# Routing 36 tiles in six groups of six instead of nine of four, over a two-group ring of rows, with GpSimd's early low halves issued in a row

## The chip, the cores and the metric

The kernel runs on one core of a Trainium2 chip. The metric is device microseconds of one execution: the median of three executions for the kernel as it is timed, and one more execution that the hardware profiler took, from which every row below comes.

## What is computed

Attention with keys and values pooled by eight feeds a mixture of eight experts with one expert per token. Cut to what matters:

```python
def reference(q, k, v, w_gate, w_output_gate, w1, w2):     # q, k, v: (8, 8, 576, 64)
    k_p = k.reshape(B, H, Sp, 8, D).mean(axis=3)           # 72 pooled keys
    v_p = v.reshape(B, H, Sp, 8, D).mean(axis=3)
    attn = softmax(q @ k_p^T / 8)
    x = (attn @ v_p).transpose(0, 2, 1, 3).reshape(4608, 512)
    logits = x @ w_gate                                    # (4608, 8)
    e_idx = argmax(logits);  gate_w = softmax(logits)[e_idx]
    eom = sigmoid(x @ w_output_gate)
    for e in range(8):                                     # w1: (8, 512, 1024), w2: (8, 1024, 512)
        mask = e_idx == e
        out[mask] = gate_w[mask] * eom[mask, e] * (relu(x[mask] @ w1[e]) @ w2[e])
```

## The kernel before

The 4608 tokens are 36 tiles of 128. The program has two parts, with a barrier of all engines between them.

**The first part** is one instruction stream that was recorded by a Python loop over `i` in 0 to 38, two halves (`a`) a step. There is no scheduler behind it: the instructions of each engine stand in the order in which the loop issued them, every engine takes its own in that order, and semaphores hold one back until what it reads is written. In half-step `a` of step `i` the loop issues the scores of tile `i` (TensorE, `scores`, L328), the transposes of the probabilities of tile `i-2` (`transpose_p`, L349, copied out by ScalarE, L350), the negated row maxima of tile `i` (VectorE, `peak`, L334, tiles `m`), the product with the values of tile `i-3` (`values`, L360), the four exponentials (ScalarE, `softmax`, L340) and the normalising of tile `i-3` into the row buffer `xg` (`normalise`, VectorE, L377 and L383). A dictionary `plan` holds other work by step: loading and pooling keys (GpSimd adds, L260, then ScalarE's `scale_k`, L265, into `kbd`), halving the values (GpSimd, L282), and so on. A row of `xg` holds a token's attention output, its id and its gate weight.

**Routing** works on a group of tiles. When the last tile of a group is normalised, `route(g)` is put into a queue two steps later; `work` then takes a few VectorE instructions from it in each half-step, among the others. The first reduces the gate columns of the group's rows (L398), some twelve small ones follow, TensorE counts ranks with 1 + n matmuls (L435, L437), and the last of them, a cast (L460), writes `where`: the place of each token in a buffer `xs` in HBM that is sorted by expert. From then on `place_ids` issues one indirect DMA (a scatter) for each tile from GpSimd's queue (L514), one a half-step; at the end of the loop whatever is left goes out at once. A group's rows in `xg` are free again when their scatters have landed. The scatters have their numbers by tile, 0 to 35.

**The first layer of expert 0** starts inside the first part. When 24 tiles are placed, `gather_early` (step 31) loads three tiles of `xs` (SyncE, L105). `turn_x` transposes each (VectorE, L110), `turn_hi` copies it to the high half of `xt` (ScalarE, L556), and `turn_lo` writes the low half (GpSimd, L560, three instructions). The early pieces of `w1` are split in the same way: `split_hi` (ScalarE, L539) and `split_lo` (GpSimd, L543, eight instructions of 128x512), at the steps in `HIGHS` and from 31.5 on every half-step. After the loop a list `TAIL` says the order by hand: `M` is a hidden chunk on TensorE (`hidden_chunk`, L732, twelve matmuls, which need the high and low halves of all three tiles), `W10` ten pieces of routing work, `Z` one more indirect DMA that puts blank rows behind the first expert's (`blank_tail`, L472), `Y` an output chunk (L738). The rank matmuls of the last group stand on TensorE behind two `M`.

**The second part** (`experts`) runs all experts by loops over jobs of two or three tiles. Before it SyncE waits until every scatter and the blank tail have landed, and all engines meet at a barrier (L1685 in the profile). Five of the eight output chunks `Y` stand before the barrier, the others behind it.

Of the kernel before, what the change touches and what calls it, by code (L numbers as in the profile page):

```python
# [10 lines left out]
F32 = mybir.dt.float32  # L11
# [11 lines left out]
P = 128  # L23
# [14 lines left out]
ROW = ID + 2  # L38
# [2 lines left out]
SENT_ID = SENT - 2  # L41
PAIRS = SENT // 2
LOADS = 4 * 16
GROUPS = (4,) * 9
TAKEN = 5
BEFORE = 31
TURNS = 33.5
SIDES = ((0, 5), (5, 3))
# [34 lines left out]
TURN = 5  # L83
FIRST = 2
HIGHS = (21, 25, 25.5, 26, 29.5, 30, 30.5, 33)
PLACED = (0, 1, 1, 2, 2, 3, 3)
SOONER = 192
CODE = 159
# [35 lines left out]
def attention_and_routing(ctx, tc, sh, qT, kT, v, wg, wst, xs):  # L124
    nc = tc.nc
    cp = ctx.enter_context(tc.tile_pool(name="cp", bufs=1))
    p2 = ctx.enter_context(tc.tile_pool(name="p2", bufs=2))
# [3 lines left out]
    def const(shape, dt, name):  # L131
        return cp.tile(shape, dt, tag=name, name=name)
# [186 lines left out]

    s_t, pT_t, xg, grec = {}, {}, {}, {}  # L320
    GMAX = max(GROUPS)
    place = [(g, j) for g, n in enumerate(GROUPS) for j in range(n)]

    def scores(i, a):
# [27 lines left out]
    def values(i, a):  # L352
        av = sh.p_y[a]
        pT = pT_t[i]
        for c, k_a, k0, k1 in side_slots():
            if k_a != a:
                continue
            o = COLS * (SLOTS[k0][2] - SIDES[a][0])
            for r0, n, b, s0 in segments(i):
                nc.tensor.matmul(av[r0:r0 + n, o:o + COLS * (k1 - k0)], pT[:, BLOCKS[0] * a + c, r0:r0 + n],  # L360
                                 vbd[b % 2][:, k0:k1].rearrange("p h f -> p (h f)"),
                                 start=(c == 0), stop=(c == BLOCKS[a] - 1), skip_group_check=True)
        g, j = place[i]
        if a == 0:
            if j == 0:
                while len(placed) < sum(GROUPS[:max(g - 2, 0)]):
                    work(1, True)
                    place_ids()
                xg[g] = p2.tile([P, GMAX, ROW], F32, tag="xg", name=f"xg{g}", bufs=3)
                n, t0 = group(g)  # L370
                nc.gpsimd.iota(xg[g][:, 0:n, ID], pattern=[[P, n]], base=t0 * P, channel_multiplier=1,
                               allow_small_or_imprecise_dtypes=True)
                grec[g] = p2.tile([P, GMAX, H], F32, tag="grec", name=f"grec{g}")
        h0, n = SIDES[a]
        hs = slice(h0, h0 + n)
        avv = av[:, 0:n * COLS].rearrange("p (h f) -> p h f", h=n)
        nc.vector.reciprocal(grec[g][:, j, hs], avv[:, :, COLS - 1])  # L377
        return avv
# [7 lines left out]
    def group(g):  # L386
        return GROUPS[g], sum(GROUPS[:g])

    def small(g, shape, dt, name):
        whole = [P, GMAX + shape[1] - GROUPS[g]] + shape[2:]  # L390
        return p2.tile(whole, dt, tag=name, name=f"{name}_{g}", bufs=1)[:, 0:shape[1]]
# [115 lines left out]
    todo, placed = [], []  # L507
# [91 lines left out]
    def at(step, f, *args):  # L599
        plan.setdefault(step, []).append((f, args))  # L600
# [8 lines left out]
    def work(n, force=False):  # L609
        while n > 0 and queue:  # L610
            for item in queue:
                if force or item[1] <= tick[0]:
                    hold = next(item[0], None)
                    if hold is None:
                        queue.remove(item)
                    else:
                        item[1] = tick[0] + hold
                        n -= 1
                    break
            else:  # L620
                return

    for b in range(1, B):
        f = S * b // P + 0.5 * (b % 2)
# [23 lines left out]
        at(18 + 3 * c, stage_in, c)  # L648
    for c in range(8):
        at(HIGHS[c], split_hi, c)  # L650
        at(31.5 + 0.5 * c, split_lo, c, 0, nc.gpsimd)
    for g in range(len(GROUPS)):
        at(sum(GROUPS[:g + 1]) + 2, lambda g: queue.append([route(g), 0, g]), g)

# [1060 lines left out]
```

## Time and profile before

| | |
|---|---|
| median of three executions | 582.61 us (580.53 to 583.93) |
| the profiled execution | 585.02 us |
| its span in the trace | 583.1 us |
| TensorE (PE) busy | 566.6 us, 97% of the span |
| VectorE (DVE), ScalarE (ACT), GpSimd (POOL) busy | 335.9, 252.9 and 238.1 us |
| granted TensorE clock, mean | 0.995 |

A busy share is a mean over both parts. The rows further down are therefore taken by stretch: from the start to about 136 us the attention loop runs in full, from there to 146 us it runs out, and the first part ends at the barrier at about 168 us. In a timeline row the columns are the start, the duration, the engine, the line, the operation with its tiles, the number of instructions merged, and in brackets how long the engine was idle before and who ended it. A q behind an engine's name is its sequencer.

### The profile page before, as it was taken

How to read it: one execution, taken by the hardware profiler on the slowest of the kernel's cores; microseconds unless marked ns; L12 is line 12 of the kernel's file. 1: busy time of each engine (PE TensorE's matmuls, PEld its weight loads, DVE VectorE, ACT ScalarE, POOL GpSimd, SP SyncE). 2: the span in 40 equal slices, each digit the busy share in tenths (PEclk: the TensorE clock that was granted, in tenths of full speed). 3: DMA queues.
4: the chain of work that ended last, by engine and by line, in shares of the span. 5: the costliest groups of instructions: out<-in, count | busy, mean ns of one | idle time of the engine just before them, and what ended most of it. 6: DMA issues, size and time to landing. Idle time of an engine off the chain costs nothing.

```text
span 583.1 us, 12099 instructions
## 1 busy us (share of the span) xinstructions
PE 566.6 (97%) x3381; PEld 513.8 (88%) x3382; DVE 335.9 (58%) x771; ACT 252.9 (43%) x686; POOL 238.1 (41%) x361
## 2 busy tenths in 40 slices
PE   6999999998989999999999999999999999999996
PEld 6899998987978989898989898898998998989895
DVE  4788898888868616688665342646263741413231
ACT  2898899996425204564444120424142420302120
POOL 6658999859625422155223131231212421212131
PEclk9899999999999999999999999999999999999999
DMA  8968899967866712589772413256132212020202
GB/s 333 331 244 299 295 373 369 337 192 207 252 179 219 242 63 59 189 265 301 261 240 95 149 28 82 46 188 183 47 87 95 60 38 69 0 72 18 63 27 73
DMA packets 50351, 97.22 MB, mean 167 GB/s; under 512 B 6686, under 2 KB 32414, under 8 KB 48608
## 3 DMA queue, kind: packets, MB, share of 16 engines
q1 hardware_dynamic: 42304, 77.18, 42.0%
q0 software_dynamic: 7968, 19.24, 9.4%
q14 instruction: 61, 0.50, 0.3%
q8 instruction: 18, 0.29, 0.2%
HBM read 75.12 MB, written 22.59 MB: 168 GB/s over the span
## 4 chain that ended last, share of the span: by engine, by line
PE 56%; issue 0%; DVE 0%; POOL 0%; DVEq 0%; POOLq 0%
PE p_y L1176 27%; PE p_h L1222 27%; PE p_h L1198 1%; PE p_y L1185 0%; PE p_h L1204 0%; PE p_y L1186 0%; POOL out L1629 0%; DVE rows L1420 0%; DVE ht L1428 0%; DVEq L911 0%; DVEq L901 0%; DVEq L1019 0%; DVEq L1008 0%; DVEq L1427 0%; DVEq L1488 0%
## 5 line engine op out<-in xcount | busy, mean ns | idle before, releaser
L1290 ACT ACTIVATE ht<-p_h 128x384 fp32r<-128x384 f32 (+1 forms) x104 | 46.7, 450 | 234.4 <-PE p_h L1222 217.5
L1629 POOL DMA_INDIRECT out<-rows,dst x41 | 43.2, 1054 | 194.1 <-DVE rows L1420 191.3
L1222 PE MATMUL p_h<-xt,w1b 128*128 128x384 f32 (+1 forms) x672 | 107.6, 320 | 0.5 <-issue 0.5
L1222 PEld LDWEIGHTS p_h<-xt,w1b 128*128 128x128 f32 x672 | 106.6, 189 | 1.5 <-issue 1.1
L1428 DVE SCALAR_TENSOR_TENSOR ht<-p_h,ht 128x384 fp32r<-128x384 f32 (+1 forms) x104 | 52.2, 503 | 92.3 <-ACT ht L1290 83.7
L1176 PE MATMUL p_y<-w2b,ht 128*128 128x512 f32 x456 | 104.8, 390 | 0.0
L1176 PEld LDWEIGHTS p_y<-w2b,ht 128*128 128x128 f32 x456 | 85.4, 188 | 17.5
L1176 PE MATMUL p_y<-w2a,ht 128*128 128x512 f32 x384 | 88.6, 390 | 0.0
L1222 PEld LDWEIGHTS p_h<-xt,w1a 128*128 128x128 f32 x576 | 84.8, 190 | 1.5 <-issue 0.7
L1222 PE MATMUL p_h<-xt,w1a 128*128 128x384 f32 (+1 forms) x576 | 85.9, 309 | 0.2
L1176 PEld LDWEIGHTS p_y<-w2a,ht 128*128 128x128 f32 x384 | 71.8, 188 | 15.0 <-issue 0.4
L1420 DVE TENSOR_SCALAR rows<-p_y,sc 128x512 f32<-128x512 f32 x37 | 27.7, 750 | 99.2 <-PE p_y L1176 91.1
L340 ACT ACTIVATE p<-p_h,m 128x72 f32<-128x72 f32 x288 | 73.0, 390 | 4.0 <-DVE m L334 3.0
L1606 POOL DMA_INDIRECT xm<-xs,src x54 | 58.0, 1073 | 26.4 <-POOL src L1602 13.5
L360 PE MATMUL p_y<-vbd,pT 128*128 128x162 f32 (+3 forms) x400 | 67.4, 319 | 0.3 <-DVE xg L383 0.2
L360 PEld LDWEIGHTS p_y<-vbd,pT 128*128 128x128 f32 (+1 forms) x400 | 54.0, 179 | 3.4 <-issue 0.7
L514 POOL DMA_INDIRECT xs<-xg,where x36 | 36.3, 1008 | 24.5 <-DVE grec L377 11.3
L260 POOL TENSOR_TENSOR kq<-kq 128x288 f32<-128x288 f32 (+1 forms) x59 | 37.4, 659 | 7.1 <-ACT p L340 3.9
L383 DVE TENSOR_TENSOR xg<-p_y,grec 128x400 f32<-128x400 f32 x72 | 36.2, 503 | 1.6
L350 ACT ACTIVATE pT<-ptr 128x384 f32<-128x384 f32 x72 | 35.7, 496 | 3.0 <-PE ptr L349 2.1
L334 DVE TENSOR_REDUCE m<-p_h 128x4 f32<-128x288 f32 x72 | 32.3, 449 | 4.4 <-PE p_h L328 1.9
L349 PE MATMUL ptr<-ident,p 128*128 128x128 f32 x180 | 32.6, 279 | 1.7 <-ACT pT L350 1.0
(191 smaller groups left out, 679.4 us busy)
## 6 DMA issues: line engine op xcount, KB each, us to landing
stage<-wst SPq DMA_DIRECT2D x64, 512.0 KB
kq<-kT SPq DMA_DIRECT2D x7, 1152.0 KB
rows<-xs SPq DMA_DIRECT2D x40, 192.0 KB
rows<-v SPq DMA_DIRECT2D x8, 768.0 KB
rows<-v SPq DMA_DIRECT2D x8, 512.0 KB
rows<-xs SPq DMA_DIRECT2D x64, 64.0 KB
q_even<-qT SPq DMA_DIRECT2D x3, 1152.0 KB
kq<-qT SPq DMA_DIRECT2D x3, 1152.0 KB
```

The lines of the kernel that those rows point to most:

```text
L260: nc.gpsimd.tensor_tensor(k[:, :, 0:w], k[:, :, 0:w], k[:, :, w:2 * w], op=ALU.add)
L340: nc.scalar.activation(pt[i % 3][:, o:o + KEYS], sv[:, h], AF.Exp, bias=m[:, h:h + 1])
L350: nc.scalar.activation(pT_t[i][:, BLOCKS[0] * a:BLOCKS[0] * a + n, :], tr[:, 0:P * n].rearrange("p (c n) -> p c n", c=n), AF.Copy)
L360: nc.tensor.matmul(av[r0:r0 + n, o:o + COLS * (k1 - k0)], pT[:, BLOCKS[0] * a + c, r0:r0 + n], vbd[b % 2][:, k0:k1].rearrange("p h f -> p ...
L383: nc.vector.tensor_tensor(view(xg[g][:, j], h0, [[H, D + 16], [1, n]]), avv[:, :, 0:D + 16].rearrange("p h f -> p f h"), grec[g][:, j, h0: ...
L514: ins = nc.gpsimd.indirect_dma_start(out=xs, out_offset=bass.IndirectOffsetOnAxis(ap=where, axis=0), in_=x.bitcast(I32), in_offset=None)
L1176: i = mm(to, ht[:, h, f, P * k:P * k + P], w[:, part, o:o + DM], start=(f == 0 and part == 0 and h == 0), stop=(f == 7 and h == 1))
L1222: i = mm(to, w[:, part, o:o + P], x, start=(d == 0 and k == 0), stop=(d == 3 and k == len(terms) - 1))
L1290: act(ht[:, 0, f, 0:n], p_h[f % 3][:, 0:n], AF.Relu).then_inc(q["hh"], 1)
L1428: nc.vector.scalar_tensor_tensor(ht[:, 1, f, 0:n], src, 0.0, ht[:, 0, f, 0:n].bitcast(F32), op0=ALU.max, op1=ALU.subtract).then_inc(q["hl" ...
L1606: nc.gpsimd.indirect_dma_start(out=xb[:, k].bitcast(I32), out_offset=None, in_=pairs_of, in_offset=bass.IndirectOffsetOnAxis(ap=src[:, k:k ...
L1629: nc.gpsimd.indirect_dma_start(out=out, out_offset=bass.IndirectOffsetOnAxis(ap=dst[:, k:k + 1], axis=0), in_=yb[2 if k == size - 1 else k ...
```

## The change

Routing takes six groups of six tiles in place of nine of four. The first 24 tiles are now groups 0 to 3, so `TAKEN` is 3 in place of 5. The rows lie in one buffer of two groups (12 tiles, as three groups of four were), and a row is written again as soon as the scatter of that one tile is through: `values` asks for the scatter of the tile twelve earlier, not for a whole group. The ids of a group (L371, an iota on GpSimd) are written with its last tile, not with its first. The table `LOWS` replaces 31.5, 32, 32.5 ... as the steps of GpSimd's eight low halves.

```diff
-GROUPS = (4,) * 9
-TAKEN = 5
+GROUPS = (6,) * 6
+TAKEN = 3
...
+LOWS = (31.5, 31.5, 32, 32, 32.5, 32.5, 33, 34)
...
     GMAX = max(GROUPS)
+    group_rows = const([P, 2, GMAX, ROW], F32, "xg")
...
         if a == 0:
-            if j == 0:
-                while len(placed) < sum(GROUPS[:max(g - 2, 0)]):
+            while g > 1 and len(placed) <= sum(GROUPS[:g - 2]) + j:
+                work(1, True)
+                place_ids()
+            n, t0 = group(g)
+            if j == n - 1:
+                while g > 1 and len(placed) < sum(GROUPS[:g - 1]):
                     work(1, True)
                     place_ids()
-                xg[g] = p2.tile([P, GMAX, ROW], F32, tag="xg", name=f"xg{g}", bufs=3)
-                n, t0 = group(g)
                 nc.gpsimd.iota(xg[g][:, 0:n, ID], pattern=[[P, n]], base=t0 * P, channel_multiplier=1,
                                allow_small_or_imprecise_dtypes=True)
+            if j == 0:
+                xg[g] = group_rows[:, g % 2]
                 grec[g] = p2.tile([P, GMAX, H], F32, tag="grec", name=f"grec{g}")
...
-        at(31.5 + 0.5 * c, split_lo, c, 0, nc.gpsimd)
+        at(LOWS[c], split_lo, c, 0, nc.gpsimd)
```

How the instructions stand on three places now. Lines from 83 on have higher numbers in the changed kernel: L514 is L520, L543 is L549, L560 is L566, L383 is L389, L460 is L466.

GpSimd at the end of the first part, before. The scatters (DMA) are tiles 25, 26 and 27 of group 6, then four of group 7 and four of group 8 (the first scatter of group 6 and four low halves stand ahead of these rows); `w1a` is a low half of a weight, `xt` the low half of a gathered tile.

```order
L514 DMA xs<-xg_1606,where_1949 38912x514
L543 TENSOR_TENSOR w1a<-stage,w1a 128x512
L514 DMA xs<-xg_1606,where_1949 38912x514
L543 TENSOR_TENSOR w1a<-stage,w1a 128x512
L371 IOTA xg_2064 128x4
L514 DMA xs<-xg_1606,where_1949 38912x514
L543 TENSOR_TENSOR w1a<-stage,w1a 128x512
L560 TENSOR_TENSOR xt<-rows,xt 128x4x128
L543 TENSOR_TENSOR w1a<-stage,w1a 128x512
L560 TENSOR_TENSOR xt<-rows,xt 128x4x128 x2
L514 DMA xs<-xg_1832,where_2160 38912x514 x4
L514 DMA xs<-xg_2064,where_2248 38912x514 x4
```

The same place now, from the first low half on; the scatters are tiles 24 to 29 of group 4 and 30 to 35 of group 5.

```order
L549 TENSOR_TENSOR w1a<-stage,w1a 128x512 x7
L220 MEMSET kbd_75 128x514
L221 MEMSET kbd_75 128x1
L549 TENSOR_TENSOR w1a<-stage,w1a 128x512
L520 DMA xs<-xg,where_1954 38912x514
L566 TENSOR_TENSOR xt<-rows,xt 128x4x128
L520 DMA xs<-xg,where_1954 38912x514
L566 TENSOR_TENSOR xt<-rows,xt 128x4x128
L520 DMA xs<-xg,where_1954 38912x514 x4
L566 TENSOR_TENSOR xt<-rows,xt 128x4x128
L375 IOTA xg 128x6
L520 DMA xs<-xg,where_2134 38912x514 x6
```

The low halves of the weights have moved ahead of the scatters, all six scatters of group 4 now stand ahead of the last `xt`, and the last group has six scatters in place of four.

VectorE near the end of the loop, before, from the second row maximum of tile 34 to the second of tile 35 (`m`); the routing rows (L398, L402, L404) begin group 7.

```order
L334 TENSOR_REDUCE m_1_2031<-p_h 128x4
L377 RECIPROCAL grec_1834<-p_y 128x3
L383 TENSOR_TENSOR xg_1832<-p_y,grec_1834 128x80x3
L110 STREAM_TRANSPOSE rows<-rows 128x4x4x32
L334 TENSOR_REDUCE m_0_2058<-p_h 128x4
L398 TENSOR_REDUCE routing<-xg_1832 128x64
L377 RECIPROCAL grec_2066<-p_y 128x5
L402 TENSOR_REDUCE mx_2068<-routing 128x4
L383 TENSOR_TENSOR xg_2064<-p_y,grec_2066 128x80x5
L404 TENSOR_TENSOR d_2069<-routing,mx_2068 128x32
L110 STREAM_TRANSPOSE rows<-rows 128x4x4x32
L334 TENSOR_REDUCE m_1_2091<-p_h 128x4
```

The same place now, from the same row maximum of tile 34 to the cast that ends the routing of group 4.

```order
L336 TENSOR_REDUCE m_1_1937<-p_h 128x4
L447 TENSOR_REDUCE routing<-ex_1851 128x6
L383 RECIPROCAL grec_1856<-p_y 128x3
L451 TENSOR_TENSOR routing<-routing,running 128x48
...
L111 STREAM_TRANSPOSE rows<-rows 128x4x4x32
L336 TENSOR_REDUCE m_0_1977<-p_h 128x4
L460 SCALAR_TENSOR_TENSOR grec__4_1946<-ez_1892,routing 128x6
L461 TENSOR_REDUCE at_1953<-routing 128x6
L383 RECIPROCAL grec_1856<-p_y 128x5
L465 RECIPROCAL xg<-grec__4_1946 128x6
L466 CAST where_1954<-at_1953 128x6
```

Where group 7 began, group 4 of the changed kernel now ends: five routing instructions (L447, L451, L452, L454, L455) stand between the two maxima, and the cast that the scatter of tile 24 waits for follows the first maximum of tile 35; before, that cast (of group 6) stood in front of the first maximum of tile 34.

GpSimd in the middle of the loop, before, around the adds (`kq`) that pool the keys of batch 3 and the values (`rows`).

```order
L260 TENSOR_TENSOR kq<-kq 128x288 x2
L514 DMA xs<-xg_290,where_565 38912x514
L260 TENSOR_TENSOR kq<-kq 128x288 x2
L514 DMA xs<-xg_290,where_565 38912x514
L260 TENSOR_TENSOR kq<-kq 128x144 x2
L514 DMA xs<-xg_290,where_565 38912x514
L260 TENSOR_TENSOR kq<-kq 128x144 x2
L514 DMA xs<-xg_290,where_565 38912x514
L260 TENSOR_TENSOR kq<-kq 128x4x72
```

The same adds now.

```order
L261 TENSOR_TENSOR kq<-kq 128x288 x4
L261 TENSOR_TENSOR kq<-kq 128x144 x4
L261 TENSOR_TENSOR kq<-kq 128x4x72
L283 TENSOR_TENSOR rows<-rows 128x64x4 x3
L520 DMA xs<-xg,where_655 38912x514
L283 TENSOR_TENSOR rows<-rows 128x64x4 x2
L520 DMA xs<-xg,where_655 38912x514 x4
```

The first group's scatters no longer stand among the adds of batch 3 but behind them.

## Rows read from the trace of the kernel before

**Rows 1.** Busy time by stretch: start:end, length, then PE, PEld, DVE, ACT, POOL.
```profile
20.00:136.00 116.00, 113.94 (x915) 104.47 (x914) 98.44 (x348) 107.08 (x420) 91.79 (x131) 1.00 0.83 295
136.00:146.00 10.00, 8.36 (x57) 7.20 (x56) 8.43 (x35) 4.59 (x16) 9.48 (x10) 1.00 0.82 236
```

**Rows 2.** Timeline of PE, from the end of attention to the second part.
```profile
143.86 0.44 PE L732 MATMUL p_h<-xt,w1a 128*128 128x384 f32 x1
145.26 4.26 PE L732 MATMUL p_h<-xt,w1a 128*128 128x384 f32 x23 [0.95 <-POOL xt L560]
...
167.94 7.79 PE L738 MATMUL p_y<-w2a,ht 128*128 128x512 f32 x33 [1.59 <-PEq L1685]
```

**Rows 3.** Timeline of POOL at the end of the first part.
```profile
130.43 0.99 POOL L514 DMA_INDIRECT xs<-xg,where  x1 [5.91 <-DVE grec L377]
...
133.51 1.00 POOL L514 DMA_INDIRECT xs<-xg,where  x1 [0.16 <-issue]
...
143.06 2.15 POOL L560 TENSOR_TENSOR xt<-rows,xt 128x512 fp32r<-128x512 f32 x2
145.52 0.99 POOL L514 DMA_INDIRECT xs<-xg,where  x1 [0.32 <-DVE where L460]
146.81 0.96 POOL L514 DMA_INDIRECT xs<-xg,where  x1 [0.30 <-issue]
...
153.14 0.96 POOL L514 DMA_INDIRECT xs<-xg,where  x1 [2.83 <-issue]
...
156.94 1.82 POOL L514 DMA_INDIRECT xs<-xg,where  x1 [0.30 <-DVE ht L594]
159.07 0.96 POOL L472 DMA_INDIRECT xs<-kbd,tail_at x1 [0.30 <-issue]
```

**Rows 4.** What SyncE's sequencer waited for: us in total, times, longest.
```profile
SPq L1685 <- DMA xs<-kbd,tail_at: 1.6, 1, 1.6
SPq L1685 <- DMA stage<-wst: 0.7, 1, 0.7
```

**Rows 5.** Groups by line: the reduction that opens a group's routing.
```profile
L398 DVE TENSOR_REDUCE routing<-xg 128x64 f32<-128x512 f32 x9 | 6.2, 684 | 0.0
```

**Rows 6.** Timeline of DVE in steps 33 to 36: routing, row maxima, turning, a late cast.
```profile
127.24 0.20 DVE L441 TENSOR_REDUCE routing<-ex 128x4 f32<-128x32 f32 x1
127.47 0.20 DVE L445 TENSOR_TENSOR routing<-routing,running 128x32 f32<-128x32 f32 x1
...
129.57 0.45 DVE L334 TENSOR_REDUCE m<-p_h 128x4 f32<-128x288 f32 x1
...
130.01 0.14 DVE L460 CAST where<-at 128x4 int32<-128x4 f32 x1
...
132.80 0.70 DVE L110 STREAM_TRANSPOSE rows<-rows 128x512 f32<-128x512 f32 x1
133.42 0.42 DVE L334 TENSOR_REDUCE m<-p_h 128x4 f32<-128x288 f32 x1
...
134.93 0.42 DVE L334 TENSOR_REDUCE m<-p_h 128x4 f32<-128x288 f32 x1
...
143.70 1.53 DVE L460 CAST where<-at 128x4 int32<-128x4 f32 x1
```

**Rows 7.** Who waited for whom: ACT's copies of pooled keys for GpSimd's adds.
```profile
ACT kbd L265 <- POOL kq L260: 3.7, 2, 1.8
```

**Rows 8.** Busy time in the two stretches around those waits, columns as in rows 1.
```profile
50.00:55.00 5.00, 4.95 (x43) 4.43 (x42) 4.07 (x18) 3.11 (x13) 4.81 (x9) 1.00 0.82 317
66.00:71.00 5.00, 5.00 (x48) 4.14 (x47) 3.98 (x19) 3.12 (x14) 4.97 (x9) 1.00 0.72 287
```

**Rows 9.** The scatters' line: time from issue to landing.
```profile
DMA to landing us min/median/max: 5.0/7.5/7.7
```

**Rows 10.** Timeline of SyncE: the early gather of three tiles.
```profile
123.08 1.87 SPq L105 DMA_DIRECT2D rows<-xs  x4
```

## The prediction

> **What bounds the kernel now.** I read the busy time by stretch first. In the attention loop, from 20 to 136 us, PE is busy for 113.94 of 116 us [rows 1]; ACT with 107.08 and DVE with 98.44 are near it but not it. All that PE lacks there is 2.06 us, so whatever the change saves on DVE, ACT or POOL in the loop cannot give back more than that. From 136 to 146 us, where the loop runs out, PE is idle for 1.64 of 10 us, and POOL, with 9.48 busy, is the fullest engine [rows 1].
>
> Then the timeline of PE at the two seams. At 143.86 it issues the first matmul of the first layer, and then stands for 0.95 us until GpSimd has written the last low half of `xt`; it goes on at 145.26 [rows 2], and POOL's row for the last two `xt` ends at 143.06 + 2.15 = 145.21 [rows 3]. So POOL's order of work at the end of the loop already sets the time there. From 145.26 on PE is never idle for long until the barrier: it is out of work at 167.94 - 1.59 = 166.35, and goes on at 167.94 [rows 2]. SyncE holds the barrier until the last indirect DMA (the blank tail, issued at 159.07 [rows 3]) and a weight load have landed: it waited 1.6 us for the one and a further 0.7 us for the other [rows 4]. Behind the barrier PE is the chain to the end, so a microsecond lost at either seam arrives at the end.
>
> **The change part by part.**
>
> *Fewer, larger groups.* The routing's small instructions on DVE, ACT and PE come six times in place of nine; the opening reduction grows from 512 to 768 elements, by its mean of 684 ns [rows 5] to about 1.0 us (an estimate, by size). On DVE this frees several us, but DVE is not what PE waits for. The bounds are a gain of 2.06 us, if all of PE's idle time in the loop were due to it, and a loss of 0.5 us, if the longer reduction or a later add holds up a row maximum. PE does not show a wait at each of the nine groups, so I take a quarter of the upper bound: **-0.5 us**.
>
> *POOL in the middle of the loop.* The first group's scatters no longer stand among the adds of batch 3. ACT waited for those adds twice, 1.84 us each time, 3.7 in total [rows 7]; these waits should go. But in the two stretches that hold them PE was busy for 4.95 and 5.00 of 5 us [rows 8]: the tiles ahead of ACT covered the wait. I cost it at nothing beyond the -0.5. With that cover gone it would be worth 3.7 us (a rival, below).
>
> *The ring.* A row is written again twelve tiles later, as before. By the order, each row's scatter is issued at least three and a half steps before the write that waits for it; a step takes 133.42 - 129.57 = 3.85 us [rows 6], so that is 13 us, and a scatter lands within 7.7 [rows 9]. Nothing waits. The checks in `values` that would force routing work find the tile placed already.
>
> *The early gather.* It needs tile 23's scatter. Group 3 now has six scatters in a row where group 5 had four, two more at 1.29 us each (145.52 to 146.81 [rows 3]), so the gather is issued at about 125.7, not 123.08 [rows 10]. Its first tile is turned at 132.80 [rows 6], so 9.7 us become 7.1, and the load itself is short of that. Cost: nothing, with 2 us or so to spare; without that cover the first layer would wait for it.
>
> *The low halves of the weights, in a row.* POOL stood idle for 5.91 us before the scatter of tile 24 [rows 3], with four low halves behind it. They now fill that gap, so POOL comes to the scatter of tile 24 with nothing else to do. That scatter, however, is late.
>
> *The last `xt`.* The scatter of tile 24 waits for the cast of group 4. Before, the cast of group 6 was at 130.01 [rows 6] and the scatter at 130.43 [rows 3], 0.28 us after the cast's end. Now I count from the second maximum of tile 34, at 133.42. Between it and the next maximum, at 134.93 [rows 6], stand five more routing instructions. Such an instruction starts 0.23 us after the one it needs (127.24, 127.47) [rows 6] and less than that after one it does not; two or three of the five need their neighbour, and I take 0.8 us for all. So the maximum is at 135.7. From a maximum to a group's cast it took 130.01 - 129.57 = 0.44 us with two instructions; there are three more now, 0.1 us each if they only follow: the cast ends at 135.7 + 0.44 + 0.3 + 0.14 = 136.6, and scatter 24 starts at 136.9. From here POOL has: scatter 0.99, `xt` 1.07, a gap of 0.16, scatter 1.00, `xt` 1.07, gap 0.16, four scatters at 1.29 but for the last gap (4.86), and the last `xt` 1.07 [rows 3]: 10.4 us, with the gaps 10.5. The last `xt` is written at **147.4**, against 145.21: PE goes on **2.1 us** later. Low bound: the five instructions cost nothing in DVE's gaps, 1.3 us. High bound: each costs a whole 0.2 and more of it stands in the way, 3.0 us. What is queued behind the scatter of tile 24 is just these `xt`, and who waits for them is PE.
>
> *The last group.* Its rank matmuls stand behind two `M` on PE, so they move with PE. Before, its first scatter started 153.14 - 145.26 = 7.9 us after PE went on; with rows half as long again I take 8.1: 155.5. From there to the blank tail it was 5.93 us (153.14 to 159.07 [rows 3]); two more scatters add 2.6. The blank tail is issued at 164.0, 4.9 us later than before and 2.8 later against PE. Of this the barrier had some to spare: SyncE's wait for the tail ended 0.7 us before its last one [rows 4]. If it lands as slowly as before, 2.1 us are exposed; if it lands in the shortest time of a scatter, 5.0 us [rows 9], and not the 6.5 or so that it had, 0.6 us. I take the middle, **+1.3 us**; bounds 0 and 2.8.
>
> On this last wait the Trainium skill has a price (DMA: Bandwidth & Descriptors, the section Anatomy of one DMA — SWDGE (gpsimd) path): about 2 us fixed and the bytes at 436 GB/s, which for a scatter of 263 KB is an estimate of 2.6 us. The trace does not agree, with a median of 7.5 [rows 9]; by the page the term would be 0 and the sum 1.6 us. The skill also says (SBUF — State Buffer, the section SBUF: two separate sides) that GpSimd cannot write a DMA's descriptors while DVE holds the port that the two share. The trace shows a scatter of 1.82 us beside DVE's `w2a` low halves where others took 0.96 [rows 3], and in the other direction a cast of 1.53 us in place of 0.14 that ended with POOL's `xt` [rows 6]. By that rule six scatters in the tail meet DVE's low halves more often than four did; a second such hit would add 0.9 us.
>
> **Sum.** -0.5 + 2.1 + 1.3 = **+2.9 us**. The profiled execution would go from 585.02 to 587.9. It stands 2.4 us above the median of the runs shown, 582.61; on the scale of the median the forecast is **585.5 us**. A difference under 0.5%, 2.9 us, is about what a measurement of this kernel cannot tell from none. So the forecast sits just on the edge between the same and slower.
>
> **The rivals.**
>
> *The seam is covered.* DVE's freed time lets the loop end earlier, PE gets back 1 to 2 of its 2.06 us, and the tail lands in time. Then +1.3 to 2.1 for the `xt`, -1.5 for the loop, 0 for the tail: 582.5 to 584, about 583.2. For it: DVE is busy for 98.44 of 116 us and loses a third of its routing. Against: PE's idle time in the loop is not at the routing.
>
> *Faster.* ACT's two waits of 1.84 us are on the path in spite of a busy PE, whose ends are modelled. Then -3.7 - 0.5 + 1.3 = -2.9: 579.7. It decides if more than 1.3 us of the 3.7 come back and the tail is hidden; to be faster beyond doubt, all must. Against it stand the two stretches of [rows 8].
>
> *More than forecast.* Scatters in runs of up to six let the adds of a later batch come late: they stand between five scatters of group 1, and ACT and then PE wait for `kbd`. With 1 us there, the high bound of 3.0 and a tail of 2.1: +5.6, 588.2.
>
> *The change does nothing*: the order rules that out; the scatters do stand ahead of the last `xt`.
>
> **How the numbers follow.** Forecast 0.60 (its own range 584 to 587.5), covered seam 0.22, faster 0.06, more than forecast 0.12. Of the forecast's share a little over half lies above 585.5, so slower has 0.36 + 0.12 = 0.48; the same has 0.24 + 0.22 = 0.46; faster has 0.06. The range that leaves out 2 in 10 reaches into the covered case and the worse one: 582.0 to 588.3.
>
> **What would show it.** Right, step by step: PE's wait for `xt` at the first layer grows from 0.95 us to 2 to 4, and POOL's last `xt` ends two us later than 145.21; the cast of group 4 stands near 136.6, and POOL is idle before scatter 24; the blank tail is issued near 164 and PE's wait at the barrier exceeds 1.59 us; ACT no longer waits for the adds of batches 3 and 4, and the start of the first layer on PE, wait left out, moves by less than 1 us. The forecast is wrong if the loop itself ends more than 1 us earlier, if the cast of group 4 falls before 135.5, or if a wait on scatters (a DVE row write, an add of keys) appears inside the loop.

## The result and the profile after

The changed kernel takes 591.31 us (median of 6, 589.95 to 592.9) where the kernel before takes 583.5 (median of 6, 580.53 to 584.11): a recorded ratio of 1.0145, with a 95% interval of 1.0123 to 1.0167 (the two medians alone give 1.0134). The forecast was 585.5 in a range of 582.0 to 588.3: slower, as it came out, but by far too little. The two profiled executions are 5.8 us apart (585.02 and 590.79), their spans 5.9 (583.1 and 589.0); that of before was longer than all six runs of its kernel. The places below are read from this pair, so they show where 5.9 of the 7.8 us between the medians lie; the other 1.9 are in no trace.

The stretches first, by the same borders as before [rows 1]: start:end, length, then PE, PEld, DVE, ACT, POOL, granted clock, DMA share, GB/s.

```profile
20.00:136.00 116.00, 114.30 (x924) 105.49 (x923) 95.79 (x312) 107.95 (x420) 93.67 (x129) 1.00 0.82 298
136.00:146.00 10.00, 6.30 (x38) 5.23 (x38) 7.18 (x23) 3.67 (x11) 8.67 (x9) 0.98 1.05 342
146.00:168.00 22.00, 21.52 (x116) 20.49 (x117) 15.07 (x65) 7.96 (x14) 9.79 (x9) 0.93 0.51 148
```

In the loop PE is a little fuller than before and DVE has 2.7 us less to do. From 136 to 146 us PE does 6.30 us in place of 8.36, and from 146 to 168 us the granted clock is 0.93, where before it was 1.00:

```profile
146.00:168.00 22.00, 20.04 (x114) 18.59 (x112) 16.87 (x72) 8.06 (x14) 9.26 (x10) 1.00 0.76 233
```

The timeline of PE at the two seams says why.

```profile
142.66 0.45 PE L738 MATMUL p_h<-xt,w1a 128*128 128x384 f32 x1
146.12 5.58 PE L738 MATMUL p_h<-xt,w1a 128*128 128x384 f32 x23 [3.01 <-POOL xt L566]
...
173.16 9.22 PE L744 MATMUL p_y<-w2a,ht 128*128 128x512 f32 x33 [4.59 <-PEq L1691]
```

Set against [rows 2]: PE comes to the first layer 1.20 us earlier (142.66 for 143.86; in both executions the first row maximum of tile 4 had been at 23.42, so the time was gained in the loop; a second profile of the kernel before, below, makes it 0.73). It then waits 3.01 us for `xt` in place of 0.95, 2.06 more, and so goes on 0.86 us later. The same 23 matmuls take 5.58 us in place of 4.26. PE is out of work at 173.16 - 4.59 = 168.57, 2.22 us later than the 166.35 before, so 1.36 us were lost between the seams. The wait at the barrier is 3.00 us longer, and the same 33 matmuls behind it take 9.22 us in place of 7.79, 1.43 more. In sum -1.20 + 2.06 + 1.36 + 3.00 + 1.43 = 6.65 us; the remaining part of the span is 0.75 us shorter, which gives the 5.9.

The 1.36 and the 1.43 are the clock. Windows of after, in the columns of the first block:

```profile
146.00:148.00 2.00, 1.88 (x6) 1.88 (x7) 0.41 (x3) 0.00 (x0) 0.16 (x2) 0.50 1.03 274
148.00:150.00 2.00, 2.00 (x11) 2.00 (x10) 0.00 (x0) 0.36 (x1) 0.00 (x0) 0.75 0.38 108
...
174.00:176.00 2.00, 2.00 (x6) 1.52 (x6) 1.93 (x4) 1.94 (x2) 1.70 (x2) 0.50 0.26 31
176.00:178.00 2.00, 2.00 (x10) 1.62 (x9) 1.73 (x6) 0.06 (x1) 1.24 (x2) 0.93 1.08 222
```

Behind each of the two waits PE has work for all of the window, and does half as much: 6 matmuls in 2 us, then 11. The level is 0.50, which is 1.2 of 2.4 GHz.

GpSimd's timeline holds the two causes.

```profile
135.55 1.00 POOL L520 DMA_INDIRECT xs<-xg,where  x1 [1.40 <-DVE where L466]
...
143.97 0.96 POOL L520 DMA_INDIRECT xs<-xg,where  x1 [0.30 <-issue]
144.96 1.10 POOL L566 TENSOR_TENSOR xt<-rows,xt 128x512 fp32r<-128x512 f32 x1
...
155.31 1.01 POOL L520 DMA_INDIRECT xs<-xg,where  x1 [9.15 <-DVE skip L505]
...
159.17 1.83 POOL L520 DMA_INDIRECT xs<-xg,where  x1 [0.31 <-DVE ht L600]
161.30 0.96 POOL L520 DMA_INDIRECT xs<-xg,where  x1 [0.30 <-issue]
162.57 1.90 POOL L520 DMA_INDIRECT xs<-xg,where  x1 [0.30 <-issue]
164.78 2.00 POOL L478 DMA_INDIRECT xs<-kbd,tail_at  x1 [0.30 <-issue]
```

The last `xt` stands behind the sixth scatter of group 4, as the order had it, and ends at 146.06. In the last group three instructions take 1.83, 1.90 and 2.00 us where one took 1.82 before [rows 3]. Just ahead of each, VectorE starts a low half of `w2a` (timeline of DVE):

```profile
158.95 1.21 DVE L549 TENSOR_TENSOR w2a<-stage,w2a 128x1024 fp32r<-128x1024 f32 x1
...
162.42 1.21 DVE L549 TENSOR_TENSOR w2a<-stage,w2a 128x1024 fp32r<-128x1024 f32 x1
...
164.72 1.22 DVE L549 TENSOR_TENSOR w2a<-stage,w2a 128x1024 fp32r<-128x1024 f32 x1
```

Each of the three GpSimd instructions ends 0.84 us behind the end of the low half that started before it; the undisturbed ones take 0.96 in all. The blank tail begins at 164.78, 5.71 us later than before, and ends 6.75 later. What SyncE waited for at the barrier (in total, times, longest) is now the tail and no weight load any more, against [rows 4]:

```profile
SPq L1691 <- DMA xs<-kbd,tail_at: 4.8, 1, 4.8
```

### The profile page after: what moved, and what is told of

Same layout as the page of the kernel before. It is cut to its first block, busy times and chain, and to the rows that moved or that the text cites. A ratio compares the mean times of both kernels' runs of the same rounds, so it can differ in the third digit from the quotient of the medians.

```text
span 589.0 us, 12023 instructions
## 1 busy us (share of the span) xinstructions
PE 566.8 (96%) x3378; PEld 515.1 (87%) x3379; DVE 330.5 (56%) x717; ACT 253.0 (43%) x680; POOL 239.8 (41%) x358
## 4 chain that ended last, share of the span: by engine, by line
PE 70%; issue 0%; POOL 0%; DVE 0%; POOLq 0%
PE p_h L1228 32%; PE p_y L1182 32%; PE p_y L744 2%; PE p_h L1204 1%; PE p_y L1191 1%; PE p_h L1210 1%; PE p_y L1192 1%; POOL out L1635 0%; DVE rows L1426 0%; POOLq L1602 0%; POOLq L1635 0%; POOLq L1604 0%
## 5 line engine op out<-in xcount | busy, mean ns | idle before, releaser
L520 POOL DMA_INDIRECT xs<-xg,where x36 | 37.2, 1035 | 27.8 <-DVE skip L505 9.2
L389 DVE TENSOR_TENSOR xg<-p_y,grec 128x400 f32<-128x400 f32 x72 | 36.2, 503 | 1.9
```

The costliest lines, as they stand in the source:

```text
L389: nc.vector.tensor_tensor(view(xg[g][:, j], h0, [[H, D + 16], [1, n]]), avv[:, :, 0:D + 16].rearrange("p h f -> p f h"), grec[g][:, j, h0: ...
L520: ins = nc.gpsimd.indirect_dma_start(out=xs, out_offset=bass.IndirectOffsetOnAxis(ap=where, axis=0), in_=x.bitcast(I32), in_offset=None)
```

## The experiments

Each time stands beside runs of the kernel before on the same chip, four chips in all; ratios carry 95% intervals.

**The kernel before, profiled again.**

> The kernel before, unedited, for a profile from the same chip as the others. Theory: PE reaches the first matmul of the first layer 120.4 us behind the row maximum of tile 4 (119.2 in the six-group kernels), waits 0.9 to 1.0 us for xt and 1.5 to 1.7 us at the barrier, with no fall of the clock behind 20 us. Rival (the profile of before was odd): either wait is over 2.5 us or absent.

583.82 us (median of 9) beside 584.98, 0.9987 (0.9969 to 1.0005). PE reaches the first layer at 143.36, 119.97 us behind the first row maximum of tile 4, waits 0.93 us for `xt` and 1.83 us at the barrier, a little more than expected, and 33 matmuls behind it take 7.77 us: full clock. The first profile was not odd, but its loop was 0.47 us slower than this one's (120.44 us to the same place).

**The seam at the first layer.** The last low half of `xt` is put ahead of three scatters of group 4:

```diff
-            if i >= NT:
+            if i > NT:
                 while todo:
                     place_ids()
```

> The changed kernel, with the last low half of xt put ahead of three of the six scatters of group 4 on GpSimd instead of behind all of them. Theory (the seam at the first layer is GpSimd's order, and a PE that stood for 3 us comes back at half clock): the last xt is written near 142 us, PE's wait there goes from 3.0 us to under 0.5, the granted clock stays at 1.00 in the stretch 146 to 150 us where it was 0.50 and 0.75, the blank tail is issued 4 to 5 us earlier, and the time falls by 4 to 5 us, to 586 to 587.5 (about 1.005 of before). The barrier's wait of 4.6 us stays. Rival (the barrier is bound by something that does not move with PE): the first layer starts early, but the wait at the barrier grows by as much, and the time falls by less than 1.5 us.

592.67 us beside 586.62, 1.0106 (1.0084 to 1.0128). The timeline of PE:

```profile
145.86 4.44 PE L738 MATMUL p_h<-xt,w1a 128*128 128x384 f32 x24
...
171.66 9.30 PE L744 MATMUL p_y<-w2a,ht 128*128 128x512 f32 x33 [4.48 <-PEq L1691]
```

The wait for `xt` is gone and 24 matmuls take 4.44 us: no half clock. The barrier's wait stays, so the rival falls. But the time fell less than the theory said, and this profile has a new hole of 2.67 us in PE near 122 us (below). The edit again, on another chip:

> The changed kernel with the last low half of xt ahead of three scatters of group 4, as in the first run of this edit, which fell on a chip where a stall of 2.8 us near 122 us disturbed three of four kernels. Theory (two seams that add): without that stall PE's wait of 3.0 us for xt and the half clock behind it (23 matmuls in 5.6 us, not 4.2) go, 4.4 us in all, the wait at the barrier stays at 4.6 to 5.0 us with its fall of the clock, and the time is 1.006 to 1.009 of before (585.5 to 587.5 where before is at 582). Rival (the seams overlap: what the first gives back the barrier takes): 1.012 to 1.015.

589.84 beside 584.98, 1.0089 (1.0057 to 1.0121). The wait at the barrier is still 4.55 us, so the seams add. This one is worth 1.0145 - 1.0089, some 0.6% or 3.3 us, if the changed kernel's ratio is the same on this chip, where it was not run; the profile has the hole near 122 us too.

The low halves in a row, undone within the change (`at(31.5 + 0.5 * c, split_lo, ...)`):

> The changed kernel with the low halves of w1a at their old steps: two of them then stand behind the scatter of tile 24, ahead of the last xt. Theory (GpSimd's row sets the seam): the last xt is 2 to 2.6 us later against the loop's end, PE's wait there 5 to 5.8 us in place of 3.0 to 3.1, with one fall of the clock as before, and the time is 2 to 2.6 us above the changed kernel, 1.018 to 1.020 of before. Rival (GpSimd waits for the cast anyway): no difference, 1.0145 to 1.0155.

595.52 beside 583.8, 1.0206 (1.018 to 1.0233), at the upper edge of what was expected. Two low halves come back behind the scatter of tile 24, and PE's row is

```profile
148.52 7.11 PE L738 MATMUL p_h<-xt,w1a 128*128 128x384 f32 x23 [5.43 <-POOL xt L566]
```

a wait 2.42 us longer than in the changed kernel, as expected, and a longer stretch at half clock: 7.11 us for what takes 4.26 at full clock. That part of the change is a gain, and so it is alone, in the kernel before:

```diff
-        at(31.5 + 0.5 * c, split_lo, c, 0, nc.gpsimd)
+        at((31.5, 31.5, 32, 32, 32.5, 32.5, 33, 34)[c], split_lo, c, 0, nc.gpsimd)
```

> The kernel before with only one part of the change: GpSimd's low halves of the weights in a row. Theory (GpSimd's order sets the start of the first layer): the low halves fill the 5.9 us in which GpSimd waited for the scatter of tile 24, the last xt is written by 142.5 us, PE's wait of 0.95 us goes, the blank tail comes 1 to 1.4 us earlier, and the time falls by 1 to 1.5 us, to 582 to 582.5 (0.997 to 0.9985 of before). Rival (the tail waits for other things): no difference, 583.2 to 583.8.

584.22 beside 586.62, 0.9966 (0.9948 to 0.9984): two us, a little more than expected, with no wait for `xt`.

**The clock.** Idle matmuls in both waits (`warm_up` writes a PSUM tile that nobody reads):

```diff
+    warm_up(14)
     for step in TAIL:
...
     while queue:
         work(1, True)
+    warm_up(12)
```

> The changed kernel with idle matmuls of 128x128 on PE in the two waits: 14 ahead of the first layer and 12 between the last output chunk and the barrier; nothing else is changed. Theory (the first layer and the first output chunks behind the barrier ran slow because the clock had fallen to half in the waits): the granted clock is 1.00 from 146 to 150 us, the 23 matmuls behind the wait take 4.3 us in place of 5.6, the 33 behind the barrier 7.8 to 8.5 in place of 9.2, and the time falls by 2 to 3 us, to 588.3 to 589.3. Rival (they ran slow for contention, with weight pieces and scatters in flight): both stay as long, and the time falls by less than 0.7 us.

595.47 beside 586.62, 1.0134 (1.0106 to 1.0162), within noise of the change itself; no gain of 2 to 3 us shows. PE, timeline:

```profile
148.99 3.29 PE L271 MATMUL warm<-ident 128*128 128x128 f32 x28
152.03 4.59 PE L740 MATMUL p_h<-xt,w1a 128*128 128x384 f32 x24
...
173.32 2.84 PE L271 MATMUL warm<-ident 128*128 128x128 f32 x24
178.22 9.38 PE L746 MATMUL p_y<-w2a,ht 128*128 128x512 f32 x33 [2.06 <-PEq L1693]
```

At the first seam the theory holds: with PE busy to the end of the wait the 24 matmuls take 4.59 us at full clock. At the barrier it does not: a wait of 2.06 us behind idle matmuls was enough for the clock to fall (9.38 us, windows of 0.50 behind it). So half of the theory's gain was not to be had. This profile also has the hole near 122 us, 2.72 us with half clock behind it, so the time alone tells nothing.

**The tail.** VectorE's four low halves of `w2a` beside the last scatters are filled with zeros instead, so the kernel leaves them out of the result:

```diff
-            split_lo(2 * 4 + split_done.pop(), 1)
+            m, h, src, hi, lo = early(2 * 4 + split_done.pop(), 1)
+            nc.vector.memset(lo.bitcast(F32), 0.0)
```

> The changed kernel with VectorE's four low halves of w2a at the end of the first part replaced by a fill with zeros of the same size (these low halves are left out of the result). Theory (the scatters of 1.8 to 2.0 us beside them are GpSimd held up by VectorE's two-input instruction): every scatter of the last group takes 0.96 to 1.0 us, the blank tail is issued 1.7 to 1.9 us earlier and ends 2.5 to 3 us earlier, PE's wait at the barrier falls from 4.6 to 1.6 to 2.5 us, and the time falls by 2 to 4 us (1.008 to 1.012 of before). Rival (those scatters are long because the queues behind them are full): two or three still take 1.8 us or more, and the time does not move by more than 0.7 us.

589.64 beside 584.98, 1.0096 (1.0064 to 1.0129). Timelines of POOL, with one of the fills on DVE, and, below, of PE:

```profile
162.07 0.96 POOL L520 DMA_INDIRECT xs<-xg,where  x1 [0.30 <-DVE ht L603]
162.10 0.91 DVE L582 MEMSET w2a<- 128x1024 f32 x1 [0.16 <-issue]
163.34 0.96 POOL L520 DMA_INDIRECT xs<-xg,where  x1 [0.30 <-issue]
164.60 0.96 POOL L520 DMA_INDIRECT xs<-xg,where  x1 [0.30 <-issue]
165.87 0.96 POOL L478 DMA_INDIRECT xs<-kbd,tail_at  x1 [0.30 <-issue]
```

```profile
148.83 5.78 PE L741 MATMUL p_h<-xt,w1a 128*128 128x384 f32 x23 [3.00 <-POOL xt L566]
...
173.44 7.78 PE L747 MATMUL p_y<-w2a,ht 128*128 128x512 f32 x33 [1.94 <-PEq L1694]
```

No scatter is above 1.01 us, the wait at the barrier is 1.94 us, and behind it the clock is whole: 33 matmuls in 7.78 us. The first seam is untouched. So the low halves are worth 2.65 us of this wait (4.59 less 1.94), and the clock behind it with them; a fill of 0.91 us beside a scatter leaves it at 0.96, so it is not merely VectorE being busy. Not all of the 2.65 us is growth: one scatter of 1.82 us stood in the kernel before as well. And the tail's own 2.00 us are not shown as a cost. With the old low halves (above) the tail took 0.96, its low half starting 0.04 us behind it, and the wait was no shorter:

```profile
168.68 0.96 POOL L478 DMA_INDIRECT xs<-kbd,tail_at  x1 [0.30 <-issue]
177.15 10.05 PE L744 MATMUL p_y<-w2a,ht 128*128 128x512 f32 x33 [4.66 <-PEq L1691]
```

From the tail's start PE went on 8.47 us later there, 8.38 in the changed kernel and 7.57 without low halves.

**Smaller groups at the end.** Groups of 6, 6, 6, 6, 4, 4, 4:

```diff
-GROUPS = (6,) * 6
+GROUPS = (6, 6, 6, 6, 4, 4, 4)
```

> The changed kernel with groups of 6, 6, 6, 6, 4, 4, 4: the first 24 tiles are as in the change, the end of the loop and the last group as before. Theory (all of the loss stands at the two seams that the large last groups make): PE starts the first layer near 143 us with a wait under 1 us, the blank tail is issued within 1 us of 157.5, the wait at the barrier is back at 1.5 to 2.2 us, no stretch after 20 us has a granted clock under 0.95, and the time is 580.5 to 583 (0.995 to 0.999 of before). Rival (large groups cost in the loop or in the second part too): it stays more than 2 us above before.

588.65 beside 586.62, 1.003 (1.0011 to 1.005): the theory's 580.5 to 583 was missed, and the 2.0 us above before are the rival's. Both seams are as before the change (waits of 0.0 and 1.25 us), but the hole of 2.64 us near 122 us is there, and DVE waits 0.9 us for a scatter since the ring is shorter for groups of four. With twelve rows counted by tiles (`xg[g] = group_rows[:, t0 % 12:t0 % 12 + n]`, and `len(placed) <= i - 12`), beside the changed kernel once more:

> Groups of 6, 6, 6, 6, 4, 4, 4 as in the earlier run, with the ring counted by tiles, so that a row is written again twelve tiles later at the end too (with two halves of six it was eight, and DVE waited 0.9 us for a scatter). Theory A: the 0.9 us go, the stall near 122 us stays with its fall of the clock, and the ratio to before is 1.001 to 1.003, against 1.003 before the edit. Theory B (the stall came of the short ring): the stall goes as well, and the ratio is 0.995 to 0.997.

> The changed kernel once more, unedited, beside the three below. In the profiles of three variants with the same loop, but not in that of the changed kernel itself, PE stood for 2.8 us near 122 to 124 us, while GpSimd was in the middle of group 3's scatters, and came back at half clock. Theory A (the stall belongs to the change and comes in most executions): it shows here, and the clocks of the timed executions lie below those of the kernel before by more than the two falls at the first layer and at the barrier explain (0.003 each). Theory B (it came from the edits or from chance): it does not show, and the ratio to before is as it was, 1.0145.

On this chip neither has the hole: 582.96 and 590.5 us beside 582.04, 1.0015 (1.0 to 1.0029) and 1.0153 (1.0121 to 1.0185). Almost the whole loss, 7.5 of 8.5 us, is undone by the end of the table of groups. The ratio is theory A's, but the stall that A kept is not there, so the run decides for neither theory. And 582.96 is 2.1 to 2.3 us above two kernels on this chip (580.9 and 580.68, below) that have the same low halves and no third and fourth group of six: these groups cost something even without the hole, and where is not shown.

Large groups at the start only, `GROUPS = (6, 6, 4, 4, 4, 4, 4, 4)`, `TAKEN = 4`, the ring by tiles, on two chips:

> The changed kernel with groups of 6, 6, 4, 4, 4, 4, 4, 4 and its ring counted by tiles (twelve rows): large groups at the start of the loop only, four scatters ahead of the early gather, the end as before. Theory A: no stall near 122 us, no fall of the clock behind 20 us, PE's start of the first layer within 1 us of that of the low halves alone, 0.995 to 0.998 of before. Theory B (large groups cost wherever they stand): above 1.000 of before.

> Groups of 6, 6, 4, 4, 4, 4, 4, 4. Theory A and B alike: no stall near 122 us, four scatters there in groups of four, 0.994 to 0.998 of before on any chip. If it stalls too, the stall is the chip's and neither the row's nor the groups'.

580.68 beside 582.04, 0.9965 (0.9945 to 0.9984); 583.11 beside 583.8, 0.9979 (0.9954 to 1.0004). PE at the seams, on the first chip:

```profile
141.74 4.46 PE L738 MATMUL p_h<-xt,w1a 128*128 128x384 f32 x24
...
164.43 7.80 PE L744 MATMUL p_y<-w2a,ht 128*128 128x512 f32 x33 [1.52 <-PEq L1691]
```

With the low halves alone (0.9966) this is the best version here, and faster than both kernels on the first chip. The gain is the low halves', which this version has too: nine groups of four with the same low halves took 580.9 and 582.58 on these two chips (below), no different from 580.68 and 583.11.

An attempt to repair both seams with a last group of two, `GROUPS = (6, 6, 6, 6, 6, 4, 2)` and the edit of the first run:

> The same edit, and the last six tiles as groups of 4 and 2 (groups of 6, 6, 6, 6, 6, 4, 2, the ring counted by tiles): the last group then has two scatters ahead of the blank tail. Theory: no wait for xt, the blank tail within 1 us of the 155.7 of the small ends, PE's wait at the barrier 1 to 2 us and no fall of the clock behind 20 us, time 0.995 to 0.998 of before: the loss of the change is then all given back, and the loop's 1.2 us and the earlier low halves are left as a gain. Rival (six-tile groups cost something that neither seam shows): 1.000 or more.

594.04 beside 584.98, 1.018 (1.0146 to 1.0214), where 0.995 to 0.998 was expected. PE, timeline:

```profile
154.27 4.44 PE L738 MATMUL p_h<-xt,w1a 128*128 128x384 f32 x24 [1.43 <-DVE ht L600]
...
164.67 8.04 PE L738 MATMUL p_h<-xt,w1a 128*128 128x384 f32 x36 [5.89 <-DVE ht L600]
```

PE no longer waits for `xt`, and only 1.25 us at the barrier, but two routings now run behind the loop, and the list `TAIL` has places for one. The rank matmuls of the last group stand between the `M`, and PE stood for 5.89 us amid the first layer. The run says nothing on the rival, only that this list is tied to the groups.

**The hole near 122 us.** PE stands for 1.2 to 2.7 us, with ACT and DVE, while GpSimd issues group 3's scatters. It is in nine of twelve profiles of kernels that have groups of six up to the early gather and these scatters in a row (on three chips; not in the changed kernel's own two), and in none of seven with other groups. Nine groups with two scatters held back, so that six stand ahead of the gather:

```diff
-            elif a or todo:
+            elif (a or todo) and not (len(placed) in (18, 19) and i < 29):
                 place_ids()
```

> Nine groups of four and the low halves in a row, as in the run of the low halves alone, but with the scatters of tiles 18 and 19 held back, so that six scatters (tiles 18 to 23) stand on GpSimd ahead of the early gather, one and then five, as in the changed kernel. Theory A (that row of scatters makes the stall, not the size of the groups): PE stands for 2 to 3 us near 121 to 124 us, the clock falls to 0.50 there, and the time is 3.5 to 4.5 us above that of the low halves alone, 1.003 to 1.005 of before. Theory B (it is the routing of six tiles on DVE and PE, or the ring): no stall, and the time is as with the low halves alone, 0.996 to 0.998 of before. Theory C: no stall there, but the early gather is later by two scatters, and DVE's first turning waits for it by up to 1 us.

580.9 beside 582.04, 0.9982 (0.9963 to 1.0001); no hole, but none of the four kernels profiled on that chip had one. So again, beside a kernel that would show it:

> Groups of 6, 6, 6, 6, 4, 4, 4 with the ring by tiles, once more, on whatever chip this is. It shows whether the chip has the stall near 122 us: with it 1.004 to 1.008 of before and PE standing for 1.4 to 2.9 us there, without it 1.000 to 1.003.

> Nine groups of four, six scatters on GpSimd ahead of the early gather. Where the first run of this job shows the stall: theory A (the row of scatters) PE stands here too, for over 1.4 us, and the time is 1.001 or more of before; theory B (the groups of six) no stall, 0.995 to 0.999. Where the first run shows none, nothing is told apart.

587.43 and 582.58 beside 583.8: 1.0062 (1.0041 to 1.0084), with a hole of 2.56 us, and 0.9976 (0.9954 to 0.9999) without. Six scatters ahead of the gather are not enough, then; but here they were through at 121.6 us, ahead of the step in which PE stalls. The last pair keeps the groups and spreads the scatters:

```diff
-LOWS = (31.5, 31.5, 32, 32, 32.5, 32.5, 33, 34)
+LOWS = (30, 30, 31.5, 31.5, 32, 32.5, 33, 34)
```

> Groups of 6, 6, 6, 6, 4, 4, 4, turning two half-steps later, and two low halves of w1a between the third and the last two of the five scatters that stand in a row ahead of the early gather. Where the second run of this job shows the stall near 122 us: theory A (scatters back to back in that step make it) PE stands there for less than 0.6 us here, and the time is 2 to 4 us below the second run's; theory B (the groups of six make it in another way) it stands for 1.2 to 2.9 us as there. Where the second shows none, nothing is told apart.

> The same with the five scatters in a row, as in the earlier runs of these groups. On a chip that has the stall PE stands for 1.2 to 2.9 us near 122 us and the ratio to before is 1.003 to 1.009; on a chip without it the ratio is 0.999 to 1.004.

584.01 and 586.22 beside 583.86: 1.0008 (0.9989 to 1.0027) broken and 1.0044 (1.0017 to 1.0072) whole. Timelines of the whole row, PE, ACT and POOL:

```profile
121.94 0.66 PE L330 MATMUL p_h<-kbd,kq 128*128 128x144 f32 x4
125.27 0.55 PE L351 MATMUL ptr<-ident,p 128*128 128x128 f32 x3 [2.68 <-ACT pT L352]
...
124.83 0.38 ACT L352 ACTIVATE pT<-ptr 128x256 f32<-128x256 f32 x1 [2.50 <-remote]
...
121.56 0.96 POOL L520 DMA_INDIRECT xs<-xg,where  x1 [0.31 <-DVE mx L408]
122.83 0.96 POOL L520 DMA_INDIRECT xs<-xg,where  x1 [0.30 <-issue]
```

and of the broken one, PE and POOL:

```profile
122.33 0.66 PE L330 MATMUL p_h<-kbd,kq 128*128 128x144 f32 x4
123.02 0.55 PE L351 MATMUL ptr<-ident,p 128*128 128x128 f32 x3
...
120.68 0.96 POOL L520 DMA_INDIRECT xs<-xg,where  x1 [0.30 <-issue]
121.66 2.51 POOL L549 TENSOR_TENSOR w1a<-stage,w1a 128x512 fp32r<-128x512 f32 x2
124.33 0.98 POOL L520 DMA_INDIRECT xs<-xg,where  x1 [0.17 <-issue]
```

PE waits for ACT, and ACT for a result of transposes that PE had issued at 120.78; the profile names no other releaser. With two low halves between the scatters the hole is gone, on a chip where the whole row has it. The 2.2 us between the medians fit too, and theory A with them: scatters back to back during that step. It is one profile of each, and the edit moves two low halves as well as it parts the scatters. What in them holds back PE's results stays open.

## Why the prediction was wrong

**The tail** is one of the two steps that failed: its term was +1.3 us with a high bound of 2.8, and PE's wait at the barrier grew by 3.00. It was mis-sized in two places. The blank tail was to be issued 2.8 us later against PE's end of work, and stands 3.49 later: it came 7.28 us ahead of that end before and 3.79 now. One more scatter than before met a low half on VectorE, for 0.94 us; the text had priced such a meeting at 0.9 us and left it out of the sum. And of that delay the term counted on getting 1.5 us back (2.8 less 1.3), by the wait for a weight load and a faster landing; 0.49 came back, since PE went on 8.87 us behind the tail's start before and 8.38 now. The tail landed 5.6 us after its issue, within the 5.0 to 6.5 that the term took; the 6.5 of the kernel before is in no trace.

That the issue time itself came near, 164.0 forecast and 164.78 measured, is luck: PE went on at 146.12, not 147.4, and from there to the tail it took 18.66 us, not 16.6, half of the excess being the half clock ahead of the last group's rank matmuls and half the long scatter.

The Trainium skill states (SBUF — State Buffer, the section SBUF: two separate sides) that a VectorE instruction with two inputs in SBUF and a GpSimd instruction that reads SBUF lock each other out of a port pair that they share, for the whole instruction. The rows agree: 1.83 to 2.00 us, ending 0.84 behind the low half, and 0.96 beside a fill.

**The clock** is the other step, and the larger miss: it was in no term, and measured 1.36 + 1.43 = 2.8 us, about as much as the whole forecast. The prediction let PE stand for about 3 us at each seam and charged only the waits. Both lengthened waits were followed by 0.50; behind the shorter ones before, the same matmuls took 4.26 and 7.79 us [rows 2]. The Trainium skill (TensorE: Matmul & The Clock Gate, Part 1: The HAM clock gate) states that the clock is set by how busy TensorE has been recently. The idle matmuls bear it out at the first seam, with 24 matmuls in 4.59 us behind them; the prediction did not weigh it.

**The last `xt`**: right in its mechanism. From the scatter of tile 24 to the end of `xt` 10.5 us were forecast and 146.06 - 135.55 = 10.51 measured; the six scatters ahead of `xt` were the cause, as moving it ahead of three of them showed. The five routing instructions between the two maxima cost 0.66 us against a forecast of 0.8. DVE, timeline of after:

```profile
131.65 0.71 DVE L111 STREAM_TRANSPOSE rows<-rows 128x512 f32<-128x512 f32 x1 [0.48 <-DMA rows<-xs]
132.29 0.42 DVE L336 TENSOR_REDUCE m<-p_h 128x4 f32<-128x288 f32 x1
...
134.46 0.42 DVE L336 TENSOR_REDUCE m<-p_h 128x4 f32<-128x288 f32 x1
...
135.15 0.13 DVE L466 CAST where<-at 128x6 int32<-128x6 f32 x1
```

All of it stands at least 1.1 us earlier than counted, since the loop itself had gained: the cast ends at 135.28, not 136.6. PE goes on 0.86 us later than before, where -0.5 + 2.1 = 1.6 were forecast.

**The loop**: -0.5 forecast, -1.2 measured in this pair (-0.7 against the second profile of before), in the right direction and within the bound of 2.06. Two of the prediction's own signs of being wrong came here, a loop that ends more than 1 us earlier and a cast before 135.5 us. Both spoke for a faster kernel, and the seams hid them. How much of the gain is the groups' is not shown: over the same distance the two profiles of one kernel, large groups at the start only, are 1.5 us apart (118.61 and 120.10).

**The early gather**: "2 us or so to spare" was too kind. It was issued at 125.98 as forecast, and DVE's first turning still waited 0.48 us for it.

**POOL in the middle of the loop**: the two waits of ACT [rows 7] did not simply go. One of 2.66 us has come in their place, at 83.98 us, and PE lost 0.73 us there. That is the mechanism of the rival "more than forecast", at a fraction of its price.

**Two slips of counting** changed no term of the sum. Behind the scatter of tile 24 the kernel before had five low halves, not four. And the covered seam's own terms (+1.3 to 2.1, -1.5 and 0) give 582.4 to 583.2, not 582.5 to 584.

**The hole near 122 us** was seen by nobody and is in neither of the two profiles of the changed kernel. Where it comes, it adds 1.2 to 2.7 us of waiting and sometimes a fall of the clock; 2.2 us lie between the medians of the last pair.

## What to carry

A long wait of PE can be priced twice: by its length, and by the work behind it at half clock; here 5.1 us of added waiting brought 2.8 us more. When indirect DMAs are the last thing ahead of a barrier, count them and look at what VectorE does beside them; it is the scatters of the last group that stand there. Large groups are cheap where nothing waits for the end of one, but brought nothing either: kept to the first two groups the edit was 0.35% faster than before on one chip and 0.2%, just within noise, on another, and GpSimd's low halves alone give as much.

## What the runs showed of the hardware

At the barrier a wait of 2.06 us, behind 2.84 us of matmuls of 128 columns, was followed by half clock, while waits of 1.25 to 1.94 us behind the output chunks were not. Waits of 2.98 to 3.01 us for `xt` were followed by it in all three profiles that have them; of the seven holes of 2.56 to 2.72 us in the loop, five were and two (2.68 and 2.69 us) were not, so the length of a wait alone does not tell. An indirect DMA on GpSimd that meets a low half already running on VectorE ends 0.82 to 0.84 us behind it (the kernel before and three profiles of its changes). And while indirect DMAs were issued back to back on GpSimd in one place of this loop, PE and the engines that wait for its results stood still on three of four chips, PE for 1.2 to 2.7 us; with two low halves between the DMAs, in one profile, they did not. The cause is open.
